# Plain float32 products in place of three rounded ones: the token reads of an attention ahead of a mixture of experts

## The chip, the cores and the metric

One core of one Trainium2 chip. The metric is the device time of one execution in microseconds (us), the median of 3 runs.

## The reference

Eight batches of 8 heads, 512 tokens of 64 numbers each, attend to 32 states per head and the states to the tokens. The 4352 result rows of 512 go through a top-1 mixture of 8 experts and then through a dense layer with a gate:

```python
scores = scale * np.matmul(x, state.transpose(0, 1, 3, 2))
a = softmax(scores)                       # shifted by the maximum, divided by sum + 1e-9
xread = np.matmul(a, state)               # the reads of the tokens
sread = np.matmul(softmax(scale * np.matmul(state, x.transpose(0, 1, 3, 2))), x)
x = concatenate([xread, sread], axis=2)   # then 4352 rows of 512
expert_idx = argmax(xn @ en.T / tau)      # rows and expert embeddings normed
out[rows of e] = gate * (relu(x @ w1[e]) @ w2[e])
h = out @ w_in
return (h * clip(h + 3, 0, 6) / 6) @ w_out
```

## The kernel before

The program is one list of operations per engine. A planner, `Sched`, makes it while the kernel is built: each operation (`op`) has a cost in us on one engine or on a choice of two, a due time, what it depends on, and which buffers it takes and gives back; the planner keeps a clock per engine and always places the operation that can start soonest, weighted with its due time. The due times in the attention are the batch's start plus an offset from the table `OFF`. Every engine then takes its list in order; a wait holds back all that stands behind it on that engine. So a changed cost or a dropped operation moves rows all through the program.

A batch of the attention (`batch`) goes like this. TensorE turns the tokens (`o_X`, xT_ps), makes the scores with the states of two groups of four heads (`o_sc`, sc_ps), turns them back (`o_sT`, s_ps). VectorE takes the row minima of the negative scores (`o_rm`, rm), subtracts them (`o_sub`, e<-s_ps,rm), ScalarE takes the exponential, VectorE the sums (rs) and reciprocals, GpSimd multiplies (`o_nm`, e<-e,rs). TensorE turns the weights (`o_aT`, L663, a_ps) and multiplies them with the states for the reads of the tokens (`o_xr`, L689, xr_ps). The result is copied to xr by ScalarE or VectorE (L692), the routing logits, eight columns that the same product makes from the states' logits, are added (`o_lg`, `o_lga`, lg), and the rows are written to memory (xd). The last batch goes in two halves of two row blocks (chunks of 512 columns in place of 1024). The reads of the states (sr, sx, sxT, xrs) go beside that.

The product for the reads is made of three rounded ones. A type that the program calls float32r takes a rounded part of a number; a high and a low part are kept of both operands: `ah` (ScalarE, L669) and `al` (VectorE, L675) of the attention weights, and `sdh` and `sdl` of the states, two tables of 128 x 528 per batch that GpSimd fills (`o_sd`, L532, L537), each state in the columns of its own head and zero elsewhere, from sth, stl (L483, L487) and gh_, gl_ (L479, L480). Three products of each pair, high x high, high x low, low x high, add up in one accumulator: 8 batches x 4 row blocks x 2 groups x 3 = 192 products of 264 columns.

Beside the attention the first pieces of w_in are converted from their stored form (`Conv`: cv_raw, cv_m, wih, wil; on VectorE L303, L304, L308 and L316, four steps). After it: the first part of the routing, 25 of 34 row columns, when the logits of batches 0 to 5 are there (L962 of 128x25 to bts, L996), the second when those of batches 6 and 7 are there (L962 of 128x9); then the index of the first five slots (pg_ps, gidx), gathers, a lead unit of five slots of the largest expert (m_g, h_g, y_g), the counts and slots of the rest (L1036 to L1077), and the main units (h_ps, y_ps) with the dense layer's products (u_ps, o) between them, until the end.

Of the kernel before, what the change touches and what calls it, by code (L numbers as in the profile page):

```python
# [8 lines left out]
F32 = mybir.dt.float32  # L9
F32R = mybir.dt.float32r  # L10
# [144 lines left out]
def kernel(  # L155
# [41 lines left out]
    def f32(ap):  # L197
        return ap.bitcast(F32)
# [17 lines left out]
    def quarters(t, g):  # L216
# [33 lines left out]
        ps=4, ax=NAX, xT=NXT, scs=NSC, e2=NE2, e1=NE1, a2=NA2, ah=NAH, al=NAH, xr=NXR, sd=2, sx=1, xs=1, acr=2,  # L250
# [4 lines left out]
    def hold(*names):  # L255
        return Hold(*(RG[n] for n in names))
# [190 lines left out]
    gh_ = one.tile([128, B, 2, E], F32R, name="gh_")  # L447
    gl_ = one.tile([128, B, 2, E], F32R, name="gl_")
    sth = one.tile([128, B, 2, D], F32R, name="sth")
    stl = one.tile([128, B, 2, D], F32R, name="stl")  # L450
# [26 lines left out]
    def o_gp(b0, b1):  # L477
        bs = slice(b0, b1)
        DVE.tensor_copy(gh_[:, bs], gq[:, bs])  # L479
        DVE.tensor_tensor(gl_[:, bs], gq[:, bs], f32(gh_[:, bs]), op=ALU.subtract)  # L480

    def o_sth(b0, b1):
        ACT.copy(sth[:, b0:b1], st[:, b0:b1])  # L483

    def o_stl(b0, b1):
        bs = slice(b0, b1)
        DVE.tensor_tensor(stl[:, bs], st[:, bs], f32(sth[:, bs]), op=ALU.subtract)  # L487
# [37 lines left out]
    def o_sd(b):  # L525
        res = []
        for s_, g_, nm in ((sth, gh_, "sdh"), (stl, gl_, "sdl")):
            t = ap2.tile([128, 2, W // 2], F32R, tag=nm, name=nm)
            for g in range(2):
                v = t[:, g].rearrange("p (h q w) -> p h q w", h=2, q=2)  # L530
                for h in range(2):
                    POOL.tensor_tensor(  # L532
                        v[:, h, :, 0:64].rearrange("p q (i a) -> p q i a", i=2),
                        f32(s_[:, b, g, :]).rearrange("p (q a) -> p q a", q=2).unsqueeze(2).to_broadcast([128, 2, 2, 32]),
                        bmask.rearrange("p (i h) -> p h i", i=2)[:, h].unsqueeze(1).unsqueeze(3).to_broadcast([128, 2, 2, 32]),
                        op=ALU.mult)
            POOL.tensor_copy(t.rearrange("p g (q w) -> p g q w", q=4)[:, :, :, 64:66],  # L537
                             f32(g_[:, b]).rearrange("p g (q i) -> p g q i", q=4))
            res.append(t)
        V["sd", b] = res  # L540
# [124 lines left out]
    def o_ah(b, r0, r1):  # L665
        if r0 == 0:
            V["ah", b] = ap1.tile([128, 2, 512], F32R, tag="ah", name="ah", bufs=NAH)
        k = slice(r0 * 128, r1 * 128)
        ACT.copy(V["ah", b][:, :, k], V["aT", b, r0][:, :, k])  # L669

    def o_al(b, r0, r1):
        if r0 == 0:
            V["al", b] = ap1.tile([128, 2, 512], F32R, tag="al", name="al", bufs=NAH)
        k = slice(r0 * 128, r1 * 128)
        DVE.tensor_tensor(V["al", b][:, :, k], V.pop(("aT", b, r0))[:, :, k], f32(V["ah", b][:, :, k]), op=ALU.subtract)  # L675

    def parts(b):
        ah, al = V["ah", b], V["al", b]
        sh, sl = V["sd", b]
        return (ah, sh), (ah, sl), (al, sh)  # L680

    def o_xr(b, r):
        if r == 0:
            V["xr", b] = big("xr").rearrange("p (r w) -> p r w", r=R) if b == B - 1 else \
                ap1.tile([128, R, W], F32, tag="xr", name="xr", bufs=NXR)
        p = V["xrp", b, r] = ps("xr_ps")
        for g in range(2):
            for i, (a, s) in enumerate(parts(b)):
                PE.matmul(p[:, g, 0:256 + E], a[:, g, r * 128:(r + 1) * 128], s[:, g, :], start=i == 0, stop=i == 2)  # L689
# [75 lines left out]
    def group(b0, b1, prio):  # L765
# [11 lines left out]
        q2 = op(lambda: o_gp(b0, b1), {"D": 0.35}, prio + 2, [q1])  # L777
        s1 = op(lambda: o_sth(b0, b1), {"A": 0.22 + 0.13 * n}, prio + 2, [ld], (), [hst])
        s2 = op(lambda: o_stl(b0, b1), {"D": 0.06 + 0.14 * n}, prio + 2, [s1], (), [hst])
        for b in range(b0, b1):  # L780
            st_ready[b], g_ready[b] = c, [q2, s2]
# [12 lines left out]
        X0c='A', X1c='*', nm='P', a2c='A', x0c='*', x1c='*', x2c='A', x3c='*', q1='A')  # L794

    PARTS = [(0, R)], [(k, k + R // 2) for k in (0, R // 2)]
    def batch(b, t, last):
# [3 lines left out]
        bscs, be2, ba2, bah, bal, bxr, bsd = (hold(n) for n in ("scs", "e2", "a2", "ah", "al", "ax" if last else "xr", "sd"))  # L801
# [40 lines left out]
        sd = do("sd", o_sd, {"P": 3.2}, g_ready[b], [bsd], port="P")  # L842
        for (r0, r1), scs in zip(chunks, scs_):
# [1060 lines left out]
```

## Time and profile before

| | |
|---|---|
| median of 3 runs | 1457.59 us (1456.26 to 1458.63) |
| the profiled execution | 1456.29 us, its span 1454.6 us |
| TensorE (PE) busy | 1349.5 us, 93% of the span, 8976 records |
| VectorE (DVE) | 917.5 us, 63% |
| ScalarE (ACT) | 598.0 us, 41% |
| GpSimd (POOL) | 433.8 us, 30% |

A row of a group tells line, engine, operation, tiles, shape and count, then the busy time in us and the mean ns of one, then the idle time of that engine just before and what ended it. A row of a timeline tells start and length in us, then the same names, and in brackets the idle time before it and its releaser. Idle time of an engine counts only where another engine or the end waits for it. A matmul's length holds its way through the array; how fast they follow one another is read from the starts.

### The profile page before, as it was taken

What the parts mean: (1) busy time and instruction counts of PE and PEld (TensorE: products, weight loads), DVE (VectorE), ACT (ScalarE), POOL (GpSimd) and SP (SyncE); (2) the same over time, 40 slices, a digit from 0 to 9 for tenths busy, and PEclk for the clock granted to TensorE, in tenths of its full rate; (3) what the DMA queues carried; (4) which work ended last, traced back from release to release, by engine and by line L of the source; (5) the groups of instructions that cost most, each with busy time, mean ns of one, the idle gap of its engine ahead of it and who ended that gap; (6) DMA issues with size and microseconds to landing.
All of it is one profiled execution on the core that took longest, in us unless ns stands there. A gap on an engine that the chain in (4) does not pass through costs nothing. (4 is left out here: it accounts for less than half of the span.)

```text
span 1454.6 us, 25083 instructions
## 1 busy us (share of the span) xinstructions
PE 1349.5 (93%) x8976; PEld 1195.2 (82%) x8976; DVE 917.5 (63%) x2108; ACT 598.0 (41%) x1290; POOL 433.8 (30%) x483
## 2 busy tenths in 40 slices
PE   7985698787789999999999999999999999999997
PEld 5765676677678898988899898998988999899996
DVE  6988777688766545655564645777867676434332
ACT  3775425455434333424333343343344444333332
POOL 5453427414143242325132133332423311100000
PEclk8998689898899999999999999999999999999999
DMA  6654326556465333334333232545554544101000
GB/s 160 169 168 141 121 70 179 156 172 190 136 190 168 95 103 105 111 92 120 119 97 114 91 117 88 173 145 159 172 153 145 163 151 141 57 23 30 16 15 15
DMA packets 151765, 175.63 MB, mean 121 GB/s; under 512 B 43785, under 2 KB 116489, under 8 KB 150609
## 3 DMA queue, kind: packets, MB, share of 16 engines
q1 hardware_dynamic: 128544, 121.19, 27.7%
q0 software_dynamic: 12336, 35.99, 8.1%
q10 hardware_dynamic: 10752, 16.78, 3.7%
q8 instruction: 73, 1.20, 0.4%
q14 instruction: 60, 0.48, 0.1%
HBM read 146.09 MB, written 27.82 MB: 120 GB/s over the span
## 5 line engine op out<-in xcount | busy, mean ns | idle before, releaser
L1650 PE MATMUL u_ps<-yh,wih 128*128 128x256 f32 x1088 | 306.5, 282 | 9.0 <-ACT yh L1626 8.1
L1650 PE MATMUL u_ps<-yw,wih 128*128 128x256 f32 x1088 | 306.5, 282 | 0.1
L1650 PE MATMUL u_ps<-yh,wil 128*128 128x256 f32 x1088 | 306.0, 281 | 0.0
L1654 ACT ACTIVATE r<-u_ps,three 128x256 f32<-128x256 f32 x272 | 129.2, 475 | 353.0 <-PE u_ps L1650 348.5
L1657 DVE SCALAR_TENSOR_TENSOR u_ps<-r,u_ps 128x256 f32<-128x256 f32 x272 | 116.4, 428 | 226.1 <-ACT r L1654 225.5
L1650 PEld LDWEIGHTS u_ps<-yh,wih 128*128 128x128 f32 x1088 | 206.7, 190 | 18.3 <-ACT yh L1626 8.3
L1685 PE MATMUL o<-woh,gh 128*128 128x512 f32 x544 | 217.0, 399 | 1.5 <-DVE yo L1699 1.2
L1685 PE MATMUL o<-wol,gh 128*128 128x512 f32 x544 | 216.1, 397 | 0.0
L1685 PE MATMUL o<-woh,gl 128*128 128x512 f32 x544 | 214.8, 395 | 0.0
L1650 PEld LDWEIGHTS u_ps<-yw,wih 128*128 128x128 f32 x1088 | 206.0, 189 | 8.5 <-DVE yw L1629 0.4
L1650 PEld LDWEIGHTS u_ps<-yh,wil 128*128 128x128 f32 x1088 | 206.6, 190 | 0.0
L1280 DVE TENSOR_TENSOR wl<-raw,wh 128x512 fp32r<-128x512 f32 x275 | 192.9, 711 | 11.3 <-ACT wh L1277 6.9
L1544 PE MATMUL y_ps<-wh,hx 128*128 128x512 f32 x512 | 185.7, 399 | 0.0
L1661 ACT CAST gh<-u_ps 128x256 fp32r<-128x256 f32 x272 | 101.4, 373 | 201.9 <-PE o L1685 162.3
L1664 DVE TENSOR_TENSOR gl<-u_ps,gh 128x256 fp32r<-128x256 f32 x272 | 114.8, 422 | 108.2 <-ACT gh L1661 107.6
L1280 POOL TENSOR_TENSOR wl<-raw,wh 128x512 fp32r<-128x512 f32 x77 | 105.3, 1368 | 245.9 <-DVE wh L1277 124.7
L1308 POOL DMA_INDIRECT xq<-xd,qidx x128 | 131.8, 1030 | 85.0 <-DVE xt L1361 34.1
L1441 PE MATMUL h_ps<-xt,wh 128*128 128x256 f32 x704 | 141.3, 290 | 1.4 <-DVE wh L1277 1.0
L1277 DVE CAST wh<-raw 128x512 fp32r<-128x512 f32 x223 | 96.4, 436 | 64.2 <-DMA raw<-in_moe_w_dram 29.4
L1704 POOL DMA_INDIRECT out_dram<-yo,ix x34 | 37.8, 1112 | 320.1 <-DVE yo L1699 219.1
L1685 PEld LDWEIGHTS o<-woh,gl 128*128 128x128 f32 x544 | 102.4, 188 | 25.1
L1441 PEld LDWEIGHTS h_ps<-xt,wh 128*128 128x128 f32 x704 | 118.1, 198 | 4.1 <-PE u_ps L1650 1.2
(307 smaller groups left out, 2342.3 us busy)
## 6 DMA issues: line engine op xcount, KB each, us to landing
raw<-in_moe_w_dram SPq DMA_DIRECT2D x176, 512.0 KB, 4.0
yl<-ysd SPq DMA_DIRECT2D x136, 64.0 KB, 2.4
xd<-xr SPq DMA_DIRECT2D x8, 1056.0 KB, 4.5
ysd<-yt POOLq DMA_DIRECT2D x32, 256.5 KB, 3.3
xb<-in_x_dram SPq DMA_DIRECT2D x48, 128.0 KB, 2.9
yw<-in_moe_w_out_dram ACTq DMA_DIRECT2D x9, 512.0 KB, 4.5
cv_raw<-in_moe_w_in_dram ACTq DMA_DIRECT2D x8, 512.0 KB, 4.6
yh<-in_moe_w_in_dram ACTq DMA_DIRECT2D x8, 512.0 KB, 4.6
```

What stands on the lines that cost most here:

```text
L1277: copy[e](pc["hi"], box["t"][:, j, :])
L1280: eng[e].tensor_tensor(pc["lo"], box["t"][:, j, :], f32(pc["hi"]), op=ALU.subtract)
L1308: POOL.indirect_dma_start(q[:, j * QW:(j + 1) * QW], None, xd_q, index(qidx[:, j, s:s + 1]))
L1441: PE.matmul(out(f), pc[w][:, (2 * c + f) * 128:(2 * c + f + 1) * 128], u.xt[a][:, 2 * j + c, 256 * hf:256 * hf + 256], start=new and c == ...
L1544: PE.matmul(u.y[i], u.ht[t][:, a, lo + 128 * i:lo + 128 * i + 128], pc[w], start=c == 0 and k == 0, stop=c == KF - 1 and k == 2)
L1650: PE.matmul(p, w, y[:, k, :], start=k == 0 and j == 0, stop=k == KD - 1 and j == 2)
L1654: ACT.activation(q["r"], q["p"], AF.Relu, bias=pool["three"][:, 0:1])
L1657: DVE.scalar_tensor_tensor(q["p"], q["r"], 6.0, q["p"], op0=ALU.min, op1=ALU.mult)
L1661: ACT.copy(q["h"], q["p"])
L1664: DVE.tensor_tensor(q["l"], q["p"], f32(q["h"]), op=ALU.subtract)
L1685: PE.matmul(o["o"][a], g[:, a * 128:(a + 1) * 128], w, start=m == 0 and j == 0, stop=m == KFF - 1 and j == 2)
L1704: POOL.indirect_dma_start(out, bass.IndirectOffsetOnAxis(ap=o["ix"][:, a:a + 1], axis=0), box["t"], None)
```

## The change

The reads of the tokens become one plain float32 product per row block and group: 64 products in place of 192, of ah (a plain copy of the turned weights, by ScalarE or VectorE as the planner chooses) with one table sd. The parts al, sdl, stl, gh_ and gl_ and their operations go; stk is a plain copy of the states where sth was a rounded one. The planner's cost of a row block's products is now 0.9 (0.66 before), of the table 1.65 (3.2 before); the due times stay.

```diff
-    gh_ = one.tile([128, B, 2, E], F32R, name="gh_")
-    gl_ = one.tile([128, B, 2, E], F32R, name="gl_")
-    sth = one.tile([128, B, 2, D], F32R, name="sth")
-    stl = one.tile([128, B, 2, D], F32R, name="stl")
+    stk = one.tile([128, B, 2, D], F32, name="stk")
...
-    def o_gp(b0, b1):
-        bs = slice(b0, b1)
-        DVE.tensor_copy(gh_[:, bs], gq[:, bs])
-        DVE.tensor_tensor(gl_[:, bs], gq[:, bs], f32(gh_[:, bs]), op=ALU.subtract)
-
-    def o_sth(b0, b1):
-        ACT.copy(sth[:, b0:b1], st[:, b0:b1])
-
-    def o_stl(b0, b1):
-        bs = slice(b0, b1)
-        DVE.tensor_tensor(stl[:, bs], st[:, bs], f32(sth[:, bs]), op=ALU.subtract)
+    def o_stk(b0, b1):
+        ACT.copy(stk[:, b0:b1], st[:, b0:b1])
...
     def o_sd(b):
-        res = []
-        for s_, g_, nm in ((sth, gh_, "sdh"), (stl, gl_, "sdl")):
-            t = ap2.tile([128, 2, W // 2], F32R, tag=nm, name=nm)
...
+        t = V["sd", b] = ap2.tile([128, 2, W // 2], F32, tag="sd", name="sd")
...
-    def o_ah(b, r0, r1):
+    def o_ah(e, b, r0, r1):
         if r0 == 0:
-            V["ah", b] = ap1.tile([128, 2, 512], F32R, tag="ah", name="ah", bufs=NAH)
+            V["ah", b] = ap1.tile([128, 2, 512], F32, tag="ah", name="ah", bufs=NAH)
         k = slice(r0 * 128, r1 * 128)
-        ACT.copy(V["ah", b][:, :, k], V["aT", b, r0][:, :, k])
-
-    def o_al(b, r0, r1):
...
+        copy[e](V["ah", b][:, :, k], V.pop(("aT", b, r0))[:, :, k])
...
         for g in range(2):
-            for i, (a, s) in enumerate(parts(b)):
-                PE.matmul(p[:, g, 0:256 + E], a[:, g, r * 128:(r + 1) * 128], s[:, g, :], start=i == 0, stop=i == 2)
+            PE.matmul(p[:, g, 0:256 + E], V["ah", b][:, g, r * 128:(r + 1) * 128], V["sd", b][:, g, :], start=True, stop=True)
...
-        X0c='A', X1c='*', nm='P', a2c='A', x0c='*', x1c='*', x2c='A', x3c='*', q1='A')
+        X0c='A', X1c='*', ah='*', nm='P', a2c='A', x0c='*', x1c='*', x2c='A', x3c='*', q1='A')
...
-        sd = do("sd", o_sd, {"P": 3.2}, g_ready[b], [bsd], port="P")
+        sd = do("sd", o_sd, {"P": 1.65}, g_ready[b], [bsd], port="P")
...
-            ah = do("ah", o_ah, {"A": ca(n)}, [aT], [bah] if r0 == 0 else (), args=rr)
-            al = do("al", o_al, {"D": cd(n)}, [ah], [bal] if r0 == 0 else (), [haT], args=rr)
+            ah = do("ah", o_ah, {"A": ca(n), "D": cd(n)}, [aT], [bah] if r0 == 0 else (), [haT], args=rr)
...
-            a = do("xr", o_xr, {"T": 0.66}, deps[r], [hp] + ([bxr] if r == 0 else []), [bah, bal, bsd], args=(r,),
+            a = do("xr", o_xr, {"T": 0.9}, deps[r], [hp] + ([bxr] if r == 0 else []), [bah, bsd], args=(r,),
```

The lists move. On VectorE, at the end of the attention, before the change (the last logits of the last batch, lg, and the last reduction, mx, with a conversion, cv_m, between the last two pairs):

```order
L699 COPY lg<-xr_ps 128x8
L700 TENSOR_TENSOR lg<-lg,xr_ps 128x8
L303 TENSOR_SCALAR cv_m<-cv_raw 128x512
L304 SCALAR_TENSOR_TENSOR cv_m<-cv_raw,cv_m 128x512
L308 SCALAR_TENSOR_TENSOR cv_m<-cv_raw,cv_m 128x512
L316 SCALAR_TENSOR_TENSOR cv_m<-cv_raw,cv_m 128x512
L699 COPY lg<-xr_ps 128x8
L700 TENSOR_TENSOR lg<-lg,xr_ps 128x8
L962 TENSOR_REDUCE mx_1883<-lg 128x9
```

The same place now, from the last copy ah (L653) on (four pairs of lg stand in a row, one is shown):

```order
L653 COPY ah<-a_ps 128x2x256
L303 TENSOR_SCALAR cv_m<-cv_raw 128x512
L304 SCALAR_TENSOR_TENSOR cv_m<-cv_raw,cv_m 128x512
L308 SCALAR_TENSOR_TENSOR cv_m<-cv_raw,cv_m 128x512
L671 COPY lg<-xr_ps 128x8
L672 TENSOR_TENSOR lg<-lg,xr_ps 128x8
...
L931 TENSOR_REDUCE mx_1673<-lg 128x9
```

Three steps of a conversion stand ahead of all four pairs, none between them, and the fourth step has moved behind the first index.

On TensorE around the first ranks (rk_ps; sx_ps is the state reads' transposes and logits) before the change:

```order
L714 MATMUL sx_ps<-ident,sx 128x128 x4
L724 MATMUL sx_ps<-enT,sxT 128x8 x4
L981 LDWEIGHTS ones
L981 MATMUL rk_ps<-hsum_163,ones 128x208
L982 LDWEIGHTS upper
L982 MATMUL rk_ps<-hot_161,upper 128x8x25
L689 MATMUL xr_ps<-sdh,ah 128x264
L689 MATMUL xr_ps<-sdl,ah 128x264
L689 MATMUL xr_ps<-sdh,al 128x264
```

and now:

```order
L686 MATMUL sx_ps<-ident,sx 128x128 x4
L950 LDWEIGHTS ones
L950 MATMUL rk_ps<-hsum_160,ones 128x208
L951 LDWEIGHTS upper
L951 MATMUL rk_ps<-hot_158,upper 128x8x25
L661 MATMUL xr_ps<-sd,ah 128x264 x2
L696 MATMUL sx_ps<-enT,sxT 128x8 x4
L661 MATMUL xr_ps<-sd,ah 128x264 x6
L647 MATMUL a_ps<-ident,e_1411 128x128 x4
L647 MATMUL a_ps<-ident,e_1513 128x128 x4
L661 MATMUL xr_ps<-sd,ah 128x264 x8
```

The ranks come ahead of the state reads' logits, and the reads of batches 6 and 7 are two groups of eight products in place of 24 each.

On VectorE behind the first index (gidx) the 22 steps from full to hi, which stood behind the lead unit's last gate, follow the first conversion now:

```order
L1072 SCALAR_TENSOR_TENSOR gidx_78<-pg_ps,gj_1740 128x5
L1187 MEMSET three 128x1
L316 SCALAR_TENSOR_TENSOR cv_m<-cv_raw,cv_m 128x512
L303 TENSOR_SCALAR cv_m<-cv_raw 128x512
L304 SCALAR_TENSOR_TENSOR cv_m<-cv_raw,cv_m 128x512
L308 SCALAR_TENSOR_TENSOR cv_m<-cv_raw,cv_m 128x512
L1005 TENSOR_SCALAR full<-cnt 128x8
L1006 TENSOR_SCALAR full<-full 128x8
```

They stand ahead of the lead unit's own work on VectorE.

## Rows read from the trace of the kernel before

**Rows 1.** The page's first line.

```profile
span 1454.6 us, 25083 instructions
```

**Rows 2.** Stretches: us, then busy time of PE, PEld, DVE, ACT, POOL, PEclk, DMA.

```profile
15.00:117.00 102.00, 89.71 (x1058) 68.69 (x1056) 83.48 (x167) 69.86 (x115) 45.86 (x97) 0.97 0.54 154
117.00:145.00 28.00, 15.00 (x136) 13.09 (x136) 23.75 (x63) 13.84 (x24) 7.09 (x6) 0.79 0.44 151
165.00:420.00 255.00, 209.27 (x1148) 180.75 (x1147) 198.15 (x452) 121.55 (x249) 94.18 (x89) 0.88 0.49 147
420.00:1454.00 1034.00, 1019.18 (x6537) 918.15 (x6535) 587.45 (x1353) 382.09 (x877) 265.59 (x256) 1.00 0.35 108
```

**Rows 3.** TensorE, timeline at five places; then the group of the narrow scores.

```profile
70.66 0.28 PE L689 MATMUL xr_ps<-sdh,ah 128*128 128x264 f32 x1
...
73.08 0.29 PE L689 MATMUL xr_ps<-sdh,al 128*128 128x264 f32 x1
...
75.39 1.03 PE L724 MATMUL sx_ps<-enT,sxT 128*128 128x8 f32 x8
76.28 0.96 PE L547 MATMUL xT_ps<-ident,xb 128*128 128x128 f32 x7
...
104.85 1.08 PE L560 MATMUL sc_ps<-xT,stT 128*64 128x256 f32 x8
105.87 1.09 PE L663 MATMUL a_ps<-ident,e 128*128 128x128 f32 x8
...
L560 PE MATMUL sc_ps<-xT,stT 128*64 128x256 f32 x16 | 2.2, 392 | 0.0
```

**Rows 4.** Groups of VectorE, 0 to 140 us.

```profile
L675 DVE TENSOR_TENSOR al<-a_ps,ah 128x1024 fp32r<-128x1024 f32 x7 | 8.6, 1223 | 0.5 <-ACT ah L669 0.3
...
L692 DVE COPY xr<-xr_ps 128x528 f32<-128x528 f32 x5 | 3.5, 692 | 1.0 <-PE xr_ps L689 0.5 <-issue 0.4
L479 DVE CAST gh__148<-gq 128x16 fp32r<-128x16 f32 (+2 forms) x3 | 2.3, 755 | 1.0 <-ACT gq L475 1.0
L487 DVE TENSOR_TENSOR stl<-st,sth 128x128 fp32r<-128x128 f32 (+2 forms) x3 | 1.5, 492 | 0.0
L480 DVE TENSOR_TENSOR gl__149<-gq,gh__148 128x16 fp32r<-128x16 f32 (+2 forms) x3 | 0.8, 275 | 0.1
```

**Rows 5.** VectorE, timeline: the two reductions of logits, the bts, the conversion.

```profile
116.98 0.36 DVE L962 TENSOR_REDUCE mx<-lg 128x25 f32<-128x200 f32 x1 [0.43 <-POOL lg L704]
...
125.52 1.96 DVE L996 TENSOR_TENSOR bts<-place,iqj 128x2048 bf16<-128x2048 bf16 x2
...
138.78 0.43 DVE L303 TENSOR_SCALAR cv_m<-cv_raw 128x512 int32<-128x512 int32 x1
139.24 0.69 DVE L304 SCALAR_TENSOR_TENSOR cv_m<-cv_raw,cv_m 128x512 int32<-128x512 int32 x1
...
141.44 0.16 DVE L699 COPY lg<-xr_ps 128x8 f32<-128x8 f32 x1
...
141.83 0.23 DVE L962 TENSOR_REDUCE mx<-lg 128x9 f32<-128x72 f32 x1
```

**Rows 6.** GpSimd and TensorE, timeline of the last batch.

```profile
130.83 2.68 POOL L625 TENSOR_TENSOR e<-e,rs 128x512 f32<-128x512 f32 x2
...
132.11 0.66 PE L663 MATMUL a_ps<-ident,e 128*128 128x128 f32 x4 [2.83 <-POOL e L625]
...
134.33 0.57 PE L689 MATMUL xr_ps<-sdh,ah 128*128 128x264 f32 x1
...
138.28 0.28 PE L689 MATMUL xr_ps<-sdh,al 128*128 128x264 f32 x1
```

**Rows 7.** VectorE, timeline: the first step of the counts, and hx behind the last.

```profile
172.48 0.15 DVE L1036 TENSOR_SCALAR full<-cnt 128x8 f32<-128x8 f32 x1
...
178.23 1.28 DVE L1464 SCALAR_TENSOR_TENSOR hx<-h_g,hx 128x512 fp32r<-128x512 f32 x2
```

**Rows 8.** TensorE's waits, 145 to 420 us: us in total, times, longest.

```profile
PE u_ps L1650 <- ACT yh L1626: 8.1, 1, 8.1
```

More of the change, by code (lines that the diff above doesn't have):

```diff
@@ L249 @@
     RG = {n: Ring(k) for n, k in dict(
-        ps=4, ax=NAX, xT=NXT, scs=NSC, e2=NE2, e1=NE1, a2=NA2, ah=NAH, al=NAH, xr=NXR, sd=2, sx=1, xs=1, acr=2,
+        ps=4, ax=NAX, xT=NXT, scs=NSC, e2=NE2, e1=NE1, a2=NA2, ah=NAH, xr=NXR, sd=2, sx=1, xs=1, acr=2,
         m=2, raw=NRAW, w=NW, wraw=NRAW, craw=2, cv=2, cvl=2, gx4=1, gp=2, gx=NGX, gps=6, row=NROW, rin=5, x=1, hx=NHX,
@@ L525, in o_sd @@
     def o_sd(b):
-        res = []
-        for s_, g_, nm in ((sth, gh_, "sdh"), (stl, gl_, "sdl")):
-            t = ap2.tile([128, 2, W // 2], F32R, tag=nm, name=nm)
[L529 to L540, printed above, removed]
+        t = V["sd", b] = ap2.tile([128, 2, W // 2], F32, tag="sd", name="sd")
+        for g in range(2):
+            v = t[:, g].rearrange("p (h q w) -> p h q w", h=2, q=2)
+            for h in range(2):
+                POOL.tensor_tensor(
+                    v[:, h, :, 0:64].rearrange("p q (i a) -> p q i a", i=2),
+                    stk[:, b, g, :].rearrange("p (q a) -> p q a", q=2).unsqueeze(2).to_broadcast([128, 2, 2, 32]),
+                    bmask.rearrange("p (i h) -> p h i", i=2)[:, h].unsqueeze(1).unsqueeze(3).to_broadcast([128, 2, 2, 32]),
+                    op=ALU.mult)
+        POOL.tensor_copy(t.rearrange("p g (q w) -> p g q w", q=4)[:, :, :, 64:66],
+                         gq[:, b].rearrange("p g (q i) -> p g q i", q=4))
     def o_X(b, v, r0, r1):
@@ L663, in o_aT @@
                 PE.transpose(p[:, g, r * 128:(r + 1) * 128], an[:, k:k + 128], ident)
-    def o_ah(b, r0, r1):
+    def o_ah(e, b, r0, r1):
         if r0 == 0:
-            V["ah", b] = ap1.tile([128, 2, 512], F32R, tag="ah", name="ah", bufs=NAH)
+            V["ah", b] = ap1.tile([128, 2, 512], F32, tag="ah", name="ah", bufs=NAH)
         k = slice(r0 * 128, r1 * 128)
-        ACT.copy(V["ah", b][:, :, k], V["aT", b, r0][:, :, k])
-    def o_al(b, r0, r1):
[L672 to L680, printed above, removed]
+        copy[e](V["ah", b][:, :, k], V.pop(("aT", b, r0))[:, :, k])
     def o_xr(b, r):
@@ L776, in group @@
         q1 = op(lambda: o_gqc(b0, b1), {"A": 0.25}, prio + 2, [q], (), [hq])
-        q2 = op(lambda: o_gp(b0, b1), {"D": 0.35}, prio + 2, [q1])
-        s1 = op(lambda: o_sth(b0, b1), {"A": 0.22 + 0.13 * n}, prio + 2, [ld], (), [hst])
-        s2 = op(lambda: o_stl(b0, b1), {"D": 0.06 + 0.14 * n}, prio + 2, [s1], (), [hst])
+        s1 = op(lambda: o_stk(b0, b1), {"A": 0.22 + 0.13 * n}, prio + 2, [ld], (), [hst])
         for b in range(b0, b1):
-            st_ready[b], g_ready[b] = c, [q2, s2]
+            st_ready[b], g_ready[b] = c, [q1, s1]
     OFF = dict(X0=0, X0c=1, X1=1, X1c=2, c0=2, c1=3, scs=5, mx=6, e2=7, r2=12, sT=6, rm=7, sub=8, ex=9, sum=10, rc=11,
@@ L800, in batch @@
         hsc, ha2, hsr = (hold("ps") for _ in range(3))
-        bscs, be2, ba2, bah, bal, bxr, bsd = (hold(n) for n in ("scs", "e2", "a2", "ah", "al", "ax" if last else "xr", "sd"))
+        bscs, be2, ba2, bah, bxr, bsd = (hold(n) for n in ("scs", "e2", "a2", "ah", "ax" if last else "xr", "sd"))
         def do(name, f, cost, *a, args=(), late=0.0, **k):
@@ L853, in batch @@
             aT = do("aT", o_aT, {"T": 0.00085 * n}, [nm], [haT], [be1], args=rr)
-            ah = do("ah", o_ah, {"A": ca(n)}, [aT], [bah] if r0 == 0 else (), args=rr)
-            al = do("al", o_al, {"D": cd(n)}, [ah], [bal] if r0 == 0 else (), [haT], args=rr)
+            ah = do("ah", o_ah, {"A": ca(n), "D": cd(n)}, [aT], [bah] if r0 == 0 else (), [haT], args=rr)
             for r in range(r0, r1):
-                deps[r] = [ah, al, sd]
+                deps[r] = [ah, sd]
         a2 = do("a2", o_a2, {"T": 0.87}, e2, [ha2], [be2])
```

## The prediction

> **What bounds the kernel now.** I read the page's first line, then the stretches by engine, then the groups of instructions in the attention, and last single rows of the timelines. In the stretches the reader is to see two regimes. From 420 us to the end TensorE is busy for 1019 of 1034 us at full clock [rows 1, 2]: it takes its products in order, nothing else limits it, so whatever the stretches ahead gain or lose reaches the end unchanged. Before that nothing is full. In the attention (15 to 117 us) TensorE is busy for 89.7 of 102 us and VectorE for 83.5, and each waits for the other in turn; at its end (117 to 145 us) VectorE is busy for 23.8 of 28 us and TensorE for 15.0, at a granted clock of 0.79 [rows 2]. There the logits of the last two batches are waited for, since no token can be routed without them. So the change is worth what it does to TensorE and VectorE up to 117 us, and to the chain that ends in the last reduction of logits, at 141.83 us [rows 5].
>
> **The products.** 192 rounded products of 264 columns become 64 plain ones. The rounded ones stand 20 steps in 2.42 us apart, from 70.66 to 73.08 us: 0.121 us each, 0.363 for three [rows 3]. The plain product of that shape is nowhere in the trace. Its nearest rows are the scores of the last batch: 16 records for 8 products, two each, so one plain product is two records. Four of those, each on half of the array's columns and 256 wide, are over in 1.02 us, from 104.85 to 105.87 [rows 3]. A record lasts 392 ns there and one starts every 128; a rounded record lasts 0.28 us and one starts every 0.121, so some 0.16 of a record is its tail, and 392 less 160 is 232, nearly two starts: two halves run side by side. A product on all columns then costs what such a pair costs, 0.51 us for 256 columns, 0.52 for 264. Lower end: if the halves ran one after another, 0.26. Upper end: the array's weights exchanged in the open, which the plain products of 8 columns bound, eight records in 0.89 us, 0.22 for two, so 0.74 [rows 3]. I take 0.52, the row that it is nearest to. Ahead of the first routing stand 48 such products: 48 x (0.52 - 0.363) = 7.5 us more TensorE (from -4.9 to +18.1).
>
> The Trainium skill (TensorE: Matmul & The Clock Gate, "Weight-path perf modes") speaks against the change at this place: the fast weight load is on only where 128 weights of a type other than FP32 are loaded. No row of this trace shows it for plain products of 128 columns and 264 wide; the nearest are the 8-column ones, 0.11 us a record. By the rule the sum would hold the upper end, +18.1 in place of +7.5.
>
> **VectorE.** Up to 117 us the new order takes away six subtractions of the low part, 6 x 1.22 = 7.3, the three low parts of the state, 1.5, the rounding and splitting of the state's logits, 2.3 + 0.8, and puts one half-batch subtraction of 128x512 behind, half of 1.22, 0.6: 12.5 us [rows 4]. It adds one whole conversion of a weight piece (5 stand there now, 4 before), which from 138.78 to 141.44 took 2.7; two xT copies from ScalarE, as wide as the subtraction, 2.4; and two xr copies, 2 x 0.69 = 1.4 [rows 4, 5]. That is 6.5, net -6.0. ScalarE gives those four copies up and takes the conversion's. GpSimd builds one table instead of two; it is busy for 45.9 of 102 us, so this is priced at nothing: what covers it is its own idle time, and it would count only where e<-e waits behind a table.
>
> **Sum up to 117 us.** TensorE has 12.3 us of idle time there (102 - 89.7) for 7.5 more, VectorE has 6.0 less to do. If VectorE alone set the pace, -6.0; if TensorE alone, +7.5 with no idle time used. TensorE idles largely because VectorE is late, so I let it use 8.5 of its 12.3: **-1.0**.
>
> **From the first reduction of logits to the end of the first bts** (116.98 to 127.48 us [rows 5]): the order drops a subtraction (1.2) and two steps of a conversion (0.43 + 0.69 = 1.1), and takes the half-batch subtraction (0.6): **-1.7**.
>
> **The tail.** From the bts to the last batch's reduction it took 141.83 - 127.48 = 14.3 us. A conversion of 2.7 us stood ahead of the last pair of logits although the last product started at 138.28 [rows 5, 6]. In the new order no whole conversion stands behind the last copy of the attention weights. VectorE has after the bts: two xrs copies and two reciprocal steps, small ones of half a pair of logits each, 4 x 0.2 = 0.8; a first pair of logits 0.4 (141.44 to 141.83); a conversion 2.7; three pairs 1.2; the copy ah, half as wide as an xT copy and about an xr copy, 0.7: 5.8. Beside that the other path is shorter: 0.8 to the reciprocal, GpSimd 1.34 (half of 2.68), transposes 0.66, a copy 0.7, which is 3.5 and their handovers [rows 6]. Then the products: eight at 0.52 are 4.2, and 24 rounded ones, 2.9 at full pace, started from 134.33 to 138.28 (4.0), so the low clock cost 1.1. With all eight behind the copy the last reduction comes at 5.8 + 4.2 + 1.1 + 0.4 = 11.5; with the first half done beside it, at 9.4. Middle 10.4: **-3.9** (from -4.9 to -2.8).
>
> **Behind the routing** I take 0: VectorE has a quarter of a conversion, its last step of 0.69, more to do, in a stretch where it idles for 56.9 of 255 us [rows 2, 5], and the lead unit's transposes now stand all ahead of its products, which delays the first and packs the rest.
>
> Sum: -1.0 - 1.7 - 3.9 = -6.6 us. The profiled execution took 1456.29 us (span 1454.6), which would become 1449.7. That execution stands 1.3 below the median, 1457.59; from the median, which is what I forecast, it is **1451.0 us**.
>
> **The rivals.**
>
> *More than that (A).* The new order moves the 22 small steps that count slots from behind the lead unit's last gate, where they held VectorE from 172.48 to 178.23 us and kept hx waiting [rows 7], to just behind the first index. If they lie there in time that is idle anyway, a further 5.7 goes: 1445.3. For it: VectorE is idle while gathers are under way. Against it: they may hold back x<-m_g, and the main units wait for weights afterwards.
>
> *Nothing (B).* The clock is low in the tail: 0.79 on the mean of 117 to 145 us [rows 2]. If the last eight plain products all run at half pace, they take 4.2 more; less the 1.1 already counted, 3.1 is lost: 1454.1, and with the conversion's last step unhidden, 0.7, it is 1454.8, within the noise. For it: TensorE idles ahead of 134.33. Against it: batch 6 has longer products now and closes that gap.
>
> *TensorE becomes the bound (C), slower.* Place: the products of the reads. At 0.74 each, 48 x (0.74 - 0.363) = 18.1; less the 8.5 of idle time, +9.6 in place of -1.0; the last batch adds 8 x 0.22 = 1.8, so 9.6 - 1.7 - 3.9 + 1.8 = +5.8: 1463.4. It decides from about 0.64 a product, where 48 x 0.277 - 8.5 + 8 x 0.12 equals the 5.6 saved behind 117 us. For it: nothing shows the weights of plain 128-column products hidden. Against it: in the scores they are.
>
> *A wait in place of the one removed (D), slower.* TensorE takes its list in order, and behind the routing one product that is listed too early stops it: u_ps waited 8.1 us for yh [rows 8]. The lists differ there from end to end. One more wait of that size gives 1459.1, two give 1467; it decides where the idle time of 45.7 us (255 - 209.3) rises by more than 6.6. Against it: there is no more work than before.
>
> **How the numbers follow.** What a measurement of this kernel can tell from no change is about 0.2%, 2.9 us. Forecast 0.45 (1447 to 1454), A 0.15 (1441 to 1447), B 0.16, C 0.11, D 0.13, of which 0.03, one wait, stays within the noise. Faster 0.45 + 0.15 = 0.60; same 0.16 + 0.03 = 0.19; slower 0.11 + 0.10 = 0.21. The range that leaves out 2 in 10 reaches from A's low end to where C and D begin to pass the other bound: 1442 to 1462, with 1447 to 1454 as the likeliest case's own.
>
> **What would show it.** Right: two records a product and a pair every 0.5 us at full clock; fewer than 4 us of TensorE idle time between 15 and 117 us; the first reduction near 116, the first bts ending near 124.8, the last reduction near 135.2; the stretch behind 420 us moved as a whole. Wrong: pairs every 0.7 us (C); the first reduction later than 118; eight products over 6 us in the tail (B); the last reduction early, but the work behind 420 us no earlier (D).

## The result, and the profile after

The changed kernel takes 1444.59 us in the median of 4 runs (1440.73 to 1447.93), the kernel before 1458.11 beside it: a ratio of 0.9902 (95% interval 0.9877 to 0.9927), 13.5 us less on the medians. Run once more beside other kernels its ratio was 0.9889 (0.9867 to 0.9912). The forecast was 1451.0, 6.6 us less. The profiled execution after took 1445.17 us; its span is 11.1 us shorter than that of before [rows 1]; the traces below are of these two executions, so they explain 11.1 us, while the ratios stand for 14 to 16. The page's totals now:

```profile
span 1443.5 us, 24914 instructions
...
PE 1349.8 (94%) x8912; PEld 1194.9 (83%) x8912; DVE 907.5 (63%) x2102; ACT 588.5 (41%) x1276; POOL 421.0 (29%) x445
```

TensorE is busy for as long as before (1349.5), so the whole 11.1 us are idle time that it no longer has. Where, is told by stretches that are cut at the same places of the program, not at the same times. The four stretches of the kernel before, from 15 us on: to the last reduction of logits, to the index of the main units (qidx), to 420 us, to the end. The columns are the stretch, its length, then busy us and instructions of PE, PEld, DVE, ACT and POOL, the granted clock, DMA share and GB/s.

```profile
15.00:141.83 126.83, 104.39 (x1192) 81.65 (x1190) 104.65 (x222) 82.60 (x136) 51.68 (x102) 0.94 0.50 148
141.83:212.74 70.91, 52.72 (x337) 45.49 (x338) 53.01 (x164) 25.21 (x58) 21.48 (x20) 0.74 0.31 103
212.74:420.00 207.26, 165.11 (x871) 142.47 (x871) 161.26 (x344) 105.95 (x216) 83.28 (x79) 0.89 0.56 168
420.00:1454.60 1034.60, 1019.18 (x6537) 918.15 (x6535) 587.45 (x1353) 382.09 (x877) 265.59 (x256) 1.00 0.35 108
```

The same stretches of the changed kernel:

```profile
15.00:134.43 119.43, 104.92 (x1128) 79.92 (x1126) 93.89 (x208) 79.12 (x131) 39.27 (x62) 0.95 0.52 153
134.43:203.03 68.60, 50.23 (x335) 43.02 (x336) 54.48 (x165) 26.80 (x62) 24.06 (x23) 0.73 0.39 123
203.03:420.00 216.97, 177.52 (x962) 155.01 (x962) 172.19 (x371) 105.72 (x219) 83.84 (x82) 0.89 0.57 172
420.00:1443.50 1023.50, 1009.67 (x6449) 910.04 (x6448) 576.12 (x1332) 374.78 (x860) 262.08 (x252) 0.99 0.35 106
```

TensorE's idle time is the length less its busy time. In the attention it falls from 22.4 to 14.5 us, in the lead unit's stretch it stays (18.2 and 18.4), from qidx to 420 it falls from 42.2 to 39.5, and behind that from 15.4 to 13.8. By their lengths the stretch up to the last reduction is 7.4 us shorter, the lead unit's 2.3, and all from qidx to the end 1.4. So two thirds of the gain come from the attention, as forecast, and a third from behind the last reduction, where the forecast had nothing.

VectorE's timeline after, at the places of [rows 5]: the two reductions, the first bts, a wait in the tail, the first index, the first of the 22 count steps, and qidx.

```profile
112.92 0.36 DVE L931 TENSOR_REDUCE mx<-lg 128x25 f32<-128x200 f32 x1 [0.45 <-POOL lg L676]
...
120.16 1.96 DVE L965 TENSOR_TENSOR bts<-place,iqj 128x2048 bf16<-128x2048 bf16 x2
...
127.58 0.69 DVE L316 SCALAR_TENSOR_TENSOR cv_m<-cv_raw,cv_m 128x512 f32<-128x512 f32 x1 [2.21 <-ACT cv_raw L312]
...
134.43 0.23 DVE L931 TENSOR_REDUCE mx<-lg 128x9 f32<-128x72 f32 x1
...
142.47 0.17 DVE L1072 SCALAR_TENSOR_TENSOR gidx<-pg_ps,gj 128x5 int32<-128x5 f32 x1
...
145.06 0.17 DVE L1005 TENSOR_SCALAR full<-cnt 128x8 f32<-128x8 f32 x1
...
203.03 0.33 DVE L1089 SCALAR_TENSOR_TENSOR qidx<-q_g,qt 128x164 int32<-128x164 f32 x1
```

The two of these that were not shown of the kernel before:

```profile
150.83 0.17 DVE L1103 SCALAR_TENSOR_TENSOR gidx<-pg_ps,gj 128x5 int32<-128x5 f32 x1
...
212.74 0.33 DVE L1120 SCALAR_TENSOR_TENSOR qidx<-q_g,qt 128x164 int32<-128x164 f32 x1
```

The first reduction comes 4.1 us earlier than before, the last 7.4, the first index 8.4, qidx 9.7. In the second profile of the same kernel they stand at 112.31, 133.44, 141.36 and 201.50: so a difference of 1.5 us between two traces is not to be read.

The new products on TensorE, a batch of eight in the middle of the attention, then the last transposes and the last eight products:

```profile
65.16 3.83 PE L661 MATMUL xr_ps<-sd,ah 128*128 128x264 f32 x16
...
128.69 0.63 PE L647 MATMUL a_ps<-ident,e 128*128 128x128 f32 x4 [1.90 <-DVE lg L671]
129.47 3.83 PE L661 MATMUL xr_ps<-sd,ah 128*128 128x264 f32 x16
```

There are two records a product, and eight products take 3.83 us at a granted clock of 1.00: 0.479 each, with the last one's way through the array in it. In a run below 16 stand in a row and take 7.39 us, so eight more add 3.56, 0.445 each. The stretches with these lines alone (PE and PEld busy, clock, DMA share, GB/s), first the rounded products of the kernel before (L689) up to the first reduction and from there to the last:

```profile
15.00:116.98 101.98, 21.41 (x144) 18.37 (x144) 0.97 0.54 154
116.98:141.83 24.85, 8.87 (x48) 8.38 (x48) 0.79 0.36 120
```

and the plain ones (L661):

```profile
15.00:112.92 97.92, 23.20 (x96) 17.63 (x96) 0.98 0.55 156
112.92:134.43 21.51, 10.45 (x32) 7.50 (x32) 0.84 0.38 139
```

Up to the first reduction 48 row-block products kept TensorE for 21.41 us in three rounded parts (0.446 each) and for 23.20 in one plain one (0.483).

Last, what TensorE waits for between 145 and 420 us (total, times, longest), in the kernel before:

```profile
PE y_ps L1544 <- DVE wl L1280: 14.7, 6, 5.4
PE h_ps L1441 <- DVE wl L1280: 8.8, 3, 5.8
```

and in the changed one:

```profile
PE h_ps L1410 <- DVE wl L1249: 23.0, 7, 5.8
PE m_g L1303 <- ACT xp L1298: 11.7, 4, 5.5
PE y_ps L1513 <- DVE wl L1249: 7.2, 2, 6.7
```

The wait of u_ps on yh [rows 8] is gone. The waits of h_ps and y_ps for the weights' low part wl have taken more room, 30.2 us in place of 23.5, and the lead unit's 20 transposes m_g, which stand in a row, wait for their gathers.

### The profile page after: what moved, and what is told of

It is laid out like the page before. It is cut to its first block, busy times and chain, and to the rows that moved or that the text cites. A ratio compares the mean times of both kernels' runs of the same rounds, so it can differ in the third digit from the quotient of the medians.

```text
span 1443.5 us, 24914 instructions
## 1 busy us (share of the span) xinstructions
PE 1349.8 (94%) x8912; PEld 1194.9 (83%) x8912; DVE 907.5 (63%) x2102; ACT 588.5 (41%) x1276; POOL 421.0 (29%) x445
## 5 line engine op out<-in xcount | busy, mean ns | idle before, releaser
L1249 POOL TENSOR_TENSOR wl<-raw,wh 128x512 fp32r<-128x512 f32 x80 | 109.5, 1369 | 252.2 <-DVE wh L1246 122.8
L1410 PE MATMUL h_ps<-xt,wh 128*128 128x256 f32 x704 | 145.9, 297 | 0.8 <-ACT wh L1246 0.6
L1246 DVE CAST wh<-raw 128x512 fp32r<-128x512 f32 x232 | 100.6, 436 | 63.2 <-PE y_ps L1513 23.0
L1410 PE MATMUL h_ps<-xt,wl 128*128 128x256 f32 x352 | 105.6, 300 | 27.8 <-DVE wl L1249 23.0
L1410 PEld LDWEIGHTS h_ps<-xt,wh 128*128 128x128 f32 x704 | 122.3, 206 | 2.8 <-ACT wh L1246 0.8
```

What stands on the lines that cost most here:

```text
L1246: copy[e](pc["hi"], box["t"][:, j, :])
L1249: eng[e].tensor_tensor(pc["lo"], box["t"][:, j, :], f32(pc["hi"]), op=ALU.subtract)
L1410: PE.matmul(out(f), pc[w][:, (2 * c + f) * 128:(2 * c + f + 1) * 128], u.xt[a][:, 2 * j + c, 256 * hf:256 * hf + 256], start=new and c == ...
```

## The experiments

Two theories stood at the start. **W**: VectorE and TensorE set the pace of the attention, and the change gains because VectorE has less to do. **O**: the planner, given other costs and steps, writes other lists, and the lists gain. The diff mixes both, so the first four runs part them: the list of one kernel with the work of the other. Every ratio below is to the kernel before in the same group of runs (medians 1464.0, 1456.2 and 1464.6 us for the three groups), and "us less" is worked out from it. The kernel before was traced only once, with the result, so places in the traces are compared across groups.

### The old list with the plain work

The planner sees the old steps; those of the low parts issue nothing.

```diff
     def o_al(b, r0, r1):
...
-        DVE.tensor_tensor(V["al", b][:, :, k], V.pop(("aT", b, r0))[:, :, k], f32(V["ah", b][:, :, k]), op=ALU.subtract)
+        pass
...
-            for i, (a, s) in enumerate(parts(b)):
-                PE.matmul(p[:, g, 0:256 + E], a[:, g, r * 128:(r + 1) * 128], s[:, g, :], start=i == 0, stop=i == 2)
+            PE.matmul(p[:, g, 0:256 + E], V["ah", b][:, g, r * 128:(r + 1) * 128], V["sd", b][:, g, :], start=True, stop=True)
```

> The order of the kernel before, row for row, with the work of the change: the planner is told the old costs and steps, but the steps of the low parts issue nothing and the products are plain. Theory W (work): the change gains because VectorE, which sets the pace of the attention together with TensorE, has 19 steps fewer, whatever the order; then the last reduction of logits comes 5 to 8 us earlier than 141.83 and the time is 1447 to 1452 us. Theory O (order): the gain of 13.5 us is mostly the new lists; then this kernel stays at 1455 to 1460 us. Both in part: 1452 to 1455.

Measured: 1456.95 us, ratio 0.9960 (0.9942 to 0.9978), 5.9 us less. The times that were expected count from a kernel before at 1458; it stood at 1464.0 here, so 5.9 less is the expectation's "both in part". The two reductions:

```profile
111.32 0.35 DVE L943 TENSOR_REDUCE mx<-lg 128x25 f32<-128x200 f32 x1
...
135.66 0.23 DVE L943 TENSOR_REDUCE mx<-lg 128x9 f32<-128x72 f32 x1
```

5.7 and 6.2 us earlier than in [rows 5]. That is W's gain in the attention, within its 5 to 8, without a row moved. But 0.4% is less than half of the gain in time.

### The new list with the rounded work

The opposite: the changed kernel's lists, with the low parts made again right behind their copies.

```diff
+        copy[e](V["ah", b][:, :, k], p[:, :, k])
+        DVE.tensor_tensor(V["al", b][:, :, k], p[:, :, k], f32(V["ah", b][:, :, k]), op=ALU.subtract)
```

> The order of the changed kernel, row for row, with the work of the kernel before put back: three rounded products, the low parts of the weights and of the state on VectorE right behind their copies, two tables on GpSimd. Theory W: VectorE is as late as before or later, since ah is now partly its own: the last reduction at 139 to 144 us, the time 1453 to 1462 us. Theory O: the lists carry the gain without the change in the work: 1445 to 1450 us, with 20 transposes in a row ahead of the lead unit's products and no wait of 8 us of u_ps on yh.

Measured: 1462.95 us, ratio 0.9987 (0.9972 to 1.0003). The last reduction came at 146.01, 4.2 us later than before, and still the time was no longer: what the new list loses in the attention with the old work, it regains behind. The traces of this group say the same: from qidx to the end 1245.6 us pass here, and 1249.2, 1250.0 and 1254.4 in the three runs with the old list. Neither theory alone stands. The work gives 0.4% in the old list, the new list nothing with the old work, both together 1.0%.

### The old list, plain products, with al kept; and the old list without al, with rounded products

In the first, the nine subtractions are issued and read by nobody. In the second, the third product repeats the second:

```diff
-        return (ah, sh), (ah, sl), (al, sh)
+        return (ah, sh), (ah, sl), (ah, sl)
```

> The order of before with plain products and one table, but with the 9 subtractions al on VectorE kept (their result is read by nobody). Leaves nothing out of the result. Theory W: 7 x 1.22 + 2 x 0.6 us of VectorE come back, so most of the gain of the old list with the plain work is lost again: 1454 to 1459 us. Rival P (the product's form or GpSimd's single table is what gains, VectorE's steps are hidden): as fast as the old list with the plain work, within 2 us.

> The order of before with rounded products, but without the 9 subtractions al: the third product takes the high part of the weights with the low table a second time, so the low part of the attention weights is left out of the reads. TensorE has as many products as before, VectorE 9 steps fewer. Theory W: most of the gain of the plain work appears without a plain product: 1449 to 1454 us. Rival P: no gain, 1456 to 1460 us.

Measured: 0.9987 (0.9967 to 1.0006) with al kept, 0.9966 (0.9949 to 0.9984) without al. The first reduction in both, in that order:

```profile
116.68 0.35 DVE L946 TENSOR_REDUCE mx<-lg 128x25 f32<-128x200 f32 x1
```

```profile
113.71 0.36 DVE L959 TENSOR_REDUCE mx<-lg 128x25 f32<-128x200 f32 x1
```

Plain products with al kept bring the first reduction 0.3 us forward, which is nothing. Taking al away brings 3.3 us with as many products on TensorE as before. Both (with the state's low parts, which went in the first of these too) bring 5.7. So VectorE's steps are what gains in the attention, and rival P falls. The times agree: al kept gives back most of the old list's gain, although the intervals overlap, and the trace with al kept is of the slowest of its 12 executions (1470.14 us). The stretch up to the first reduction, in the same order:

```profile
15.00:116.68 101.68, 93.06 (x1010) 68.52 (x1008) 79.44 (x159) 69.25 (x114) 32.06 (x57) 0.97 0.53 152
15.00:113.71 98.71, 90.07 (x1058) 69.53 (x1056) 77.18 (x161) 69.35 (x114) 45.70 (x97) 0.96 0.55 158
```

With al kept VectorE is busy for 4.0 us less than before [rows 2] and TensorE for 3.4 us more. That the one took what the other gave is an argument, but the next run bears it out: the plain products are not free.

### The products twice

```diff
-            PE.matmul(p[:, g, 0:256 + E], V["ah", b][:, g, r * 128:(r + 1) * 128], V["sd", b][:, g, :], start=True, stop=True)
+            for _ in range(2):
+                PE.matmul(p[:, g, 0:256 + E], V["ah", b][:, g, r * 128:(r + 1) * 128], V["sd", b][:, g, :], start=True, stop=True)
```

> The changed kernel, row for row, with each of the 64 plain products issued twice (the second overwrites the first): 64 x 0.458 = 29.3 us more TensorE, 22 of it ahead of the first reduction. If TensorE is the bound of the attention once VectorE is relieved, the first reduction comes 14 to 20 us later than 112.92 and the end 18 to 26 us later than the changed kernel's. If VectorE still sets the pace and TensorE has room: 4 to 10 us later, of which 3.7 are the last batch's eight products.

Measured: ratio 1.0073 (1.0049 to 1.0097), 25 us above the changed kernel's 0.9902 (22.7 by the spans of the two traces). The products of a batch, now 16 in a row; the work on the tile xr_ps up to the first reduction (PE, PEld, DVE, ACT); and the first reduction:

```profile
72.02 7.39 PE L662 MATMUL xr_ps<-sd,ah 128*128 128x264 f32 x32
```

```profile
15.00:130.31 115.31, 44.54 (x192) 35.91 (x192) 4.23 (x6) 10.77 (x18) 0.98 0.46 133
```

```profile
130.31 0.36 DVE L932 TENSOR_REDUCE mx<-lg 128x25 f32<-128x200 f32 x1 [0.45 <-POOL lg L677]
```

48 more products kept TensorE for 44.54 - 23.20 = 21.3 us up to the first reduction, which came 17.4 later. For a step of this size TensorE is all but the bound of the attention once VectorE is relieved: rival C named a real mechanism, and its 0.74 us a product would by this slope have eaten the gain, which is an estimate. The price was wrong, not the place.

### The copy ah on ScalarE alone

```diff
-        X0c='A', X1c='*', ah='*', nm='P', a2c='A', x0c='*', x1c='*', x2c='A', x3c='*', q1='A')
+        X0c='A', X1c='*', ah='A', nm='P', a2c='A', x0c='*', x1c='*', x2c='A', x3c='*', q1='A')
```

TensorE's list behind the lead unit's first products is that of the changed kernel; the 20 transposes ahead of them fall apart into 12, 4 and 4.

> The changed kernel with the copy ah held to ScalarE (the planner had the choice of two). Behind the lead unit's first products TensorE's list is row for row that of the changed kernel; ahead of them the lead unit's transposes stand as 12, 4 and 4 between its products in place of 20 in a row. Theory L (the 20 transposes in a row delay the lead unit and so cost time): the first lead product comes 3 to 6 us sooner behind the last reduction than the 24.7 us of the changed kernel, and the time is 2 to 5 us below it, 1.1 to 1.3% below the kernel before. Rival M (the main units' weights set the end of that stretch; the lead unit only moves its waits): the same time as the changed kernel within 2 us, 0.9 to 1.1% below the kernel before.

Measured: 0.9915 (0.9890 to 0.9940), the changed kernel's time. The first lead product, and the last one of this stretch that waits for VectorE, here and then in the changed kernel:

```profile
153.94 0.56 PE L1410 MATMUL h_g<-x,wh 128*128 128x256 f32 x1
...
184.79 0.38 PE L1410 MATMUL h_g<-x,wh 128*128 128x256 f32 x1 [0.54 <-DVE hx L1433]
```

```profile
159.14 0.56 PE L1410 MATMUL h_g<-x,wh 128*128 128x256 f32 x1
...
184.77 0.39 PE L1410 MATMUL h_g<-x,wh 128*128 128x256 f32 x1 [1.48 <-DVE hx L1433]
```

The first starts at 153.94 in place of 159.14, and qidx still comes at 203.04, the changed kernel's 203.03. One part of why is that VectorE hands over hx at the same time in both, 184.8. Another is the clock: here the 5.2 us lie at the lower one, in which both kernels are until about 162.5. This run first, then the changed kernel:

```profile
157.50:162.50 5.00, 3.93 (x17) 3.30 (x17) 4.33 (x20) 3.85 (x13) 3.01 (x5) 0.50 0.15 46
```

```profile
157.50:162.50 5.00, 4.13 (x20) 4.11 (x21) 3.89 (x14) 2.73 (x10) 2.84 (x3) 0.50 0.29 104
```

The order of the lead unit's transposes costs nothing that this run shows. From the first index to qidx 60 to 62 us pass: 61.9 before, 60.6 after, 59.8 here, 62.1 with doubled products. The next group tries what sets that.

### The planner's old costs

```diff
-        sd = do("sd", o_sd, {"P": 1.65}, g_ready[b], [bsd], port="P")
+        sd = do("sd", o_sd, {"P": 3.2}, g_ready[b], [bsd], port="P")
...
-            a = do("xr", o_xr, {"T": 0.9}, deps[r], [hp] + ([bxr] if r == 0 else []), [bah, bsd], args=(r,),
+            a = do("xr", o_xr, {"T": 0.66}, deps[r], [hp] + ([bxr] if r == 0 else []), [bah, bsd], args=(r,),
```

> The changed kernel with the planner told the old costs of the products (0.66 a row block in place of 0.9) and of the table (3.2 in place of 1.65). The work is that of the change; the list of TensorE behind the routing is nearly the same, the lists in the attention differ. If the planner's numbers carry part of the gain: 2 to 6 us above the changed kernel. If the work and the order behind the routing carry it: within 2 us of it, 0.8 to 1.1% below the kernel before.

Measured: 0.9947 (0.9929 to 0.9965), some 7 us above the changed kernel (0.9902, 0.9889), which did not run in this group; the run with ah on ScalarE did, at 0.9915. The first reduction came at 112.78, as in the changed kernel, the last at 137.72 and qidx at 206.47, each 3.3 to 3.4 later. So two numbers that issue no instruction carry some 0.3 to 0.6% of the 1.0%, and what the trace shows of it lies in the tail. The new ones are the truer: 0.9 for a row block's two products, which take two times 0.48, where the old list had 0.66.

### u_ps held back in the kernel before

```diff
-        (F1 if w == 1 else F2)(i, m, t, gated(i, t))
+        (F1 if w == 1 else F2)(i, m, t, gated(i, t) + ([RUN[0].l1] if (w, i, m) == (1, 0, 0) else []))
```

> The kernel before in all its work, with one rule more for the planner: the dense layer's first products u_ps stand behind all 96 products h_ps of the first main unit, as in the list of the changed kernel, in place of behind 72 of them. The wait of u_ps on yh of 8.1 us goes. Theory M1 (that wait was lost time, and its absence in the changed kernel is what it gained behind the routing): 5 to 8 us below the kernel before. Rival M2 (TensorE waits for weights wl in that stretch whatever stands in it; the wait moves to h_ps and y_ps): within 2 us of the kernel before.

Measured: 0.9971 (0.9957 to 0.9985), 4.2 us less: more than M2 allows, less than M1 expected. The wait on yh is gone, and between 145 and 420 us waits of h_ps for wl stand in its place, 17.8 us where the kernel before has 8.8 (y_ps has 11.1 in place of 14.7):

```profile
PE h_ps L1441 <- DVE wl L1280: 17.8, 6, 8.7
```

So the wait moved, as M2 says, and the time fell all the same. The same rule was tried in the next group, on another list, and there it lost.

### The tail without conversions, alone and with that rule

```diff
-        b = op(lambda: c.ca(ma), {"D": 0.96}, prio, [a], [hc], port="D")
+        b = op(lambda: c.ca(ma), {"D": 0.96}, prio, [a, *wait], [hc], port="D")
...
-            convert(n, CV0 + CVR * n, early, early_m, start=16.01)
+            convert(n, CV0 + CVR * n, early, early_m, start=16.01, wait=lga_[B - 1] if n >= 5 else ())
```

> The changed kernel with the sixth and later conversions of w_in held back until the last logits: seven conversion steps that stood on VectorE between the first bts and the last reduction go behind it (the list behind the routing then has u_ps behind 72 of the 96 products h_ps again, as in the kernel before). In the changed kernel one of these steps waits 2.21 us for ScalarE and holds back logits, and TensorE waits 1.90 us for them. If those conversions set the tail: the last reduction at 130 to 132.3 us in place of 134.43, and the time 2 to 4 us below the changed kernel unless the wait of u_ps on yh comes back and gives some 4 us away. If they stand in time that is idle anyway: 134 to 135 us.

> The same as the run without the conversions in the tail, and u_ps held behind all 96 products h_ps of the first main unit. Theory M1 (the wait of u_ps on yh is lost time): 3 to 5 us below the run without that rule, and 1.1 to 1.4% below the kernel before. Rival M2 (the wait only moves to the weights): the same within 2 us.

Measured: 0.9839 (0.9815 to 0.9862) for the first, faster than both kernels; 0.9880 (0.9860 to 0.9900) with the rule on u_ps. In the first:

```profile
132.25 0.23 DVE L931 TENSOR_REDUCE mx<-lg 128x9 f32<-128x72 f32 x1
...
206.36 0.33 DVE L1089 SCALAR_TENSOR_TENSOR qidx<-q_g,qt 128x164 int32<-128x164 f32 x1
```

The last reduction is 2.2 us earlier, as expected. But the conversions are then done behind it, and qidx comes 3.3 later than in the changed kernel. The end is 6.6 us earlier in the profiles all the same (span 1436.9), and the interval lies wholly below the changed kernel's 0.9867 to 0.9912 beside it. So that gain is not the one that was expected: it arises behind qidx, where TensorE's waits for wl are shorter, 22.2 us in place of the changed kernel's 30.2. The waits of TensorE behind qidx there:

```profile
PE y_ps L1513 <- DVE wl L1249: 11.1, 5, 6.0
PE h_ps L1410 <- DVE wl L1249: 11.1, 6, 5.0
PE u_ps L1619 <- ACT yh L1595: 7.5, 1, 7.5
```

and with the rule:

```profile
PE y_ps L1513 <- DVE wl L1249: 10.2, 8, 3.1
PE h_ps L1410 <- ACT wh L1246: 9.4, 2, 7.9
PE h_ps L1410 <- DVE wl L1249: 8.8, 5, 4.1
```

The wait of 7.5 us on yh goes and one of 7.9 on wh stands in its place: here too the wait moved, and the time rose by 0.4%. That the moved wait made the loss is not shown: of the 9.4 us between the two spans (1436.9 and 1446.3) 1.0 lies ahead of qidx and 8.4 more than 220 us behind it. The fastest list of all has the wait on yh in it. So M1 does not hold in general.

### More VectorE work behind the last gate

```diff
+        if i:
+            for _ in range(4):
+                DVE.tensor_tensor(t[:, 3], eq, obf[:, 0].unsqueeze(1).to_broadcast([128, n, NTILE]), op=ALU.mult)
```

> The changed kernel, row for row, with one step of at of 1394 columns, 0.87 to 0.90 us on VectorE, issued four times more ahead of the index of the main units: 3.5 us more VectorE behind the last gate of the lead unit. Theory V (between the first index and the main units' index VectorE's chain of gates, counts, at and es sets the pace, which is why 60 to 62 us pass there in every run and the order of the lead unit's transposes does not matter): qidx 2.5 to 3.5 us later than 203.03 and the time 2 to 4 us above the changed kernel. Rival (TensorE's own products or the weights set it): qidx within 1 us, the time the same.

Measured: 0.9904 (0.9884 to 0.9924), not to be told from the 0.9889 of the changed kernel run beside it.

```profile
188.61 0.58 PE L1413 MATMUL h_g<-x,wh 128*128 128x256 f32 x1 [4.90 <-DVE hx L1436]
...
195.80 10.17 PE L1069 MATMUL pg_g<-at,bts 128*128 128x164 bf16 x34
...
208.88 0.33 DVE L1092 SCALAR_TENSOR_TENSOR qidx<-q_g,qt 128x164 int32<-128x164 f32 x1
```

The products for the index of the main units, pg_g, in the changed kernel:

```profile
189.53 10.17 PE L1066 MATMUL pg_g<-at,bts 128*128 128x164 bf16 x34
```

qidx comes 5.9 us later than in the first profile of the changed kernel for the 4.6 us that the four steps took. So work that is added to VectorE there reaches qidx, and the run without conversions in the tail points the same way: VectorE is busy for 60.95 us between the last reduction and qidx in place of 54.48, and the stretch takes 74.1 us in place of 68.6. But VectorE alone does not set it. Behind the last gate of the lead unit, at 163.2 us in the changed kernel, it works without a pause up to hx, for which TensorE waits until 184.77; then TensorE runs the rest of its lead products and pg_g, 10.17 us, and VectorE waits 4.4 us for these. With the added steps TensorE waits 4.90 us for hx, and the same lead products behind that wait take 7.2 us at a granted clock of 0.62 in place of 4.8 at 1.00: these 2.4 us are why the delay is longer than the added work.

Whether the time followed, as the second half of theory V says, is open. The ratios differ by 2.2 us, with an uncertainty of about 4; in the traces from qidx to the end the same 1240 us pass (1240.1, and 1240.5 in the changed kernel), so there the end followed.

### The changed kernel again

> The changed kernel once more, nothing edited, beside the others: 0.9 to 1.1% below the kernel before, as the first time (0.73 to 1.23%). If it is only 0.5 to 0.7% below, then the changed kernel and the one with the planner's old costs do not differ.

Measured: 0.9889 (0.9867 to 0.9912). The gain holds, and the old costs do differ.

## Why the prediction was right, and where it was not

The forecast was right in its direction, its likeliest mechanism and its range; the time came out at 1444.6 where 1451.0 was forecast, outside the likeliest case's own 1447 to 1454 and inside rival A's 1441 to 1447. That it lies in the range at all is in part luck, since what went beyond the forecast came from no cause that it had priced. By its own steps:

**What bounds the kernel: right.** TensorE's busy time did not move, behind 420 us TensorE is busy for 98.6% of the stretch (98.5% before), and the attention's gain is there: the last reduction at 134.43, forecast near 135.2. That these two are so near is luck in part: -1.0, -1.7 and -3.9 were forecast, -4.1, -1.3 and -2.0 came.

**The products: mis-sized.** "I take 0.52 ... 7.5 us more TensorE". A plain product took 0.445 to 0.479 at full clock, which is near. The larger error lay in the other operand of the difference: 0.363 is the rounded triple's pace in one full-clock stretch of 20 steps [rows 3], while over the attention a triple kept TensorE for 0.446. The difference of the two means, 0.483 - 0.446, times 48 is 1.8 us. An estimate of the new cost was set against the best case of the old one. No exchange of weights stands in the open, as the row of the scores had suggested: the weight loads of the plain products last 203 ns, those of the rounded ones 204 to 207, and the 16 loads of the last eight products lie beside these, 3.41 us from 129.46 on:

```profile
L661 PEld LDWEIGHTS xr_ps<-sd,ah 128*128 128x128 f32 x128 | 25.1, 203 | 11.2 <-ACT ah L653 4.7 <-issue 2.2
```

The Trainium skill (TensorE: Matmul & The Clock Gate, "Weight-path perf modes") keeps the fast weight load for types other than FP32. By that rule the prediction's sum would have held +18.1. The trace does not bear that price out: the loads here are no longer than the rounded ones' and are covered. The same page ("Step-by-step: what each phase is for") says that the next weights load while the present product runs, and with that these rows agree.

**VectorE: right.** The forecast was 6.0 less up to the first reduction; it was busy for 83.5 us up to there [rows 2] and is for 76.9 now, 6.6 less. And the two runs on al show that these steps move the first reduction forward, not the new form of the products.

**The sum up to 117 us: mis-sized by the term before.** "-1.0" was -4.1. With +1.8 in place of +7.5 little had to be hidden; the idle time of TensorE between 15 us and the first reduction did not shrink below 4 us, as the text wanted to see, but only from 12.3 to 8.5.

**To the end of the first bts: right.** The forecast was -1.7; it took 10.50 us before and 9.20 after, -1.3.

**The tail: mis-sized the other way.** "-3.9" was -2.0 (14.35 to 12.31). That "no whole conversion stands behind the last copy of the attention weights" was true, but one stands ahead of it, and its last step waits 2.21 us for ScalarE, with three pairs of logits behind it and TensorE's transposes waiting 1.90 for those. Without the conversions the tail falls by 2 us more. The low clock that the forecast feared for the last products (rival B) was not there for the last eight: 3.83 us, at a granted clock of 1.00 from 129.4 to 133.4 us. It was there for the eight ahead of them, which took the rest of the 10.45 us, 6.6: the granted clock was 0.50 from 119.0 to 121.6 us and 0.60 from there to 126.2.

**Behind the routing: the step that failed.** "I take 0." In the profiles it is 11.1 - 7.4 = 3.7 us, 2.3 ahead of qidx and 1.4 behind it; by the ratios, 14 to 16 us in all, it is 7 to 9. The old list with the plain work shows how to read that: its last reduction came 6.2 us earlier and its time fell by 5.9, very near the forecast's 6.6, so nothing clear of its interval (3 to 8 us) came behind. What lies beyond is the new lists' own. Most of it lies behind qidx: the old list with the plain work has qidx at 204.11, only 1.1 us after the changed kernel, and is 8 to 10 us slower by the ratios. Rival A had the sign, not the cause: the 22 count steps did move into the time of the gathers (145.06, before in [rows 7]), yet from the first index to qidx only 1.3 us went (61.9 to 60.6), and the old list with the plain work takes 59.5 there with these steps in their old place. Rival D's wait did go, but the two runs with the rule on u_ps show that such a wait can be taken out and come back as another, once beside a gain and once beside a loss. What in the lists behind qidx makes 4 to 10 us stays open; with the same products and steps, lists that differed in a planner's number or in one rule gave ratios of 0.984, 0.988, 0.990, 0.995 and 0.996.

## What to carry to other kernels

Where a planner writes the order, part the change from its new order before pricing either: run the old list with the new work and the new list with the old work. Set a new cost against the mean that the old one has in place, with its slow stretches, not against its best row. A wait that can be named is not yet a loss: try it on two lists before believing in it.

## What the runs showed of the hardware

A plain float32 product of 128 columns and 264 wide came as two records and took 0.445 us at full clock where 16 stood in a row; the rounded product of that shape took 0.121 [rows 3], so one plain product takes as long as 3.7 rounded ones, and three rounded ones at full clock stay cheaper on TensorE; it was VectorE's share of making the parts that made them dear. Lead products that were started 5.2 us sooner found the clock at 0.50 until 162.5 us as the later ones did, and brought nothing forward. A wait of 4.90 us on TensorE was followed by 7.2 us at a granted clock of 0.62, for products that took 4.8 at 1.00 behind a wait of 1.48. Four steps of 1394 columns on VectorE took 4.59 us in a row where single ones take 0.87; why is not shown.
